# RetNet attention and a gated MLP on one core: the late tokens in blocks of 512, both layers by 26 products, sums of W_out streamed from DRAM

## The chip, the cores and the metric

The kernel runs on one core of a Trainium2 chip. The metric is the device time of one execution, in microseconds. A core has five engines that run their own instruction streams in order and wait for each other by semaphores: TensorE (PE in the profile; PEld are its weight loads), VectorE (DVE), ScalarE (ACT), GpSimd (POOL) and SyncE (SP), which here only issues DMAs. Data lie in SBUF, products land in PSUM, inputs and outputs are in DRAM.

## The reference

```python
# q, k, v: (4, 8, 768, 64) float32; the weights are float64
for t in range(768):
    state = gamma * state + k[:, :, t] (outer) v[:, :, t]     # per head, 64 x 64
    y[:, :, t] = scale * q[:, :, t] @ state
x = y as (3072 tokens, 512)
h = x @ w_in                                   # w_in (512, 2048)
g = h * erf(softplus(h))
out = g @ w_out                                # w_out (2048, 512)
```

All 3072 x 512 outputs are computed in float32. The weights arrive as float64 words and are turned into float32 on the chip.

## The kernel before

Tokens are cut into 24 chunks of 128 (`j`), six to a batch. Attention works by chunks: scores inside a chunk, the state of 64 x 64 per head carried from chunk to chunk. The decays are multiplied into keys and queries beforehand (`prepared`, L575: keys by rows, keys and queries in blocks of 32, then two 32 x 32 block transposes on VectorE).

*The first 512 tokens* (groups g = 0 to 3, G0 = 4) use plain products: `hidden` (L901) makes four feature tiles of 512 columns, `project` (L921) multiplies them by W_out, while VectorE and ScalarE still convert the weights.

*The late 2560 tokens* go in ten pieces of 256 (SCH), each in two halves s of the features: 20 groups g = 4 to 23. In `hidden_steps` (L978) the first layer is a fast product scheme, 26 products in place of 32 (`STEPS`), each as two matmuls of 128 columns; four PSUM banks are read, added into `h` by VectorE (L999) or first written by ScalarE (L1001, L1003), and used again. The sums of x that the products need are made by `x_sums` (L957, 18 a piece), those of W_in once by `sum_in` (L381, 30 a half). The second layer is a seven-product scheme (`PRODUCTS`, `project_part`, L1058): four gated sums a group (`g_sums`, L1040, VectorE), the sums of W_out made once by a ScalarE copy and an accumulating DMA from GpSimd (`sums`, L388), the products gathered in PSUM and combined by `put_part` (L1084). So the order of the late work is written out by hand in the loop at L1266: within a group, 26 steps of the first layer, three output products of the group before among them, then softplus (`gate_softplus`), the visit of one attention chunk (`sub_visit`, L755: its own additions and the scores of the next chunk), erf, four more output products, and gating.

*DMAs.* Everything but the accumulating ones is issued by SP in program order. `load(j)` (L195) brings a late chunk by 34 DMAs: keys and values whole (L208, L218), queries and keys once more as 16 small DMAs of 16 KB each (`load_blocks`, L184, issued at L190), because the block transposes want 32 x 32 blocks in place. `kq` and `v` have three buffers, `kb` two, so the load of chunk j waits until the visit of chunk j - 3 is over. In the loop `load(j + 3)` follows each visit.

```python
for s, d in itertools.product(range(2), range(2)):      # load_blocks, L187 to L193
    part = slice((2 * s + d) * 32, (2 * s + d + 1) * 32)
    for u in range(HP):
        nc.sync.dma_start(to[part, u * C : (u + 1) * C]..., src[2 * u + s, :, d * 32 : (d + 1) * 32]...)
```

Of the kernel before, what the change touches and what calls it, by code (L numbers as in the profile page):

```python
# [22 lines left out]
P = 128  # L23
C = 128
# [9 lines left out]


OUT = {"11": 0, "12": 1, "21": 2, "22": 3, "T3": 1, "T1": 4, "T2": 5, "T4": 6}

PRODUCTS = {
    1: ("11", "11"), 2: ("12", "21"), 3: ("S4", "22"), 4: ("22", "T4"),
    5: ("S1", "T1"), 6: ("S2", "T2"), 7: ("S3", "T3"),  # L40
}

# [60 lines left out]
    (10, 14, 2, True, ((3, True),)),  # L106
    (22, 0, 3, True, ((5, True),)),
    (23, 7, 0, False, ((5, True),)),
    (24, (0, 1), 1, False, ((7, False),)),
    (25, 15, 2, False, ((2, True),)),  # L110
    (14, (2, 1), 3, False, ((7, True),)),
    (9, 8, 0, False, ((7, True),)),
    (12, 6, 1, False, ((6, False),)),
    (2, 11, 2, True, ((2, False), (6, True))),
    (17, 1, 3, True, ((2, False), (4, True))),
    (15, 10, 0, False, ((6, True),)),
    (8, 9, 1, False, ((4, False),)),
    (3, 4, 0, False, ()),
    (19, (1, 0), 0, False, ((0, True),)),
    (7, 13, 1, False, ((2, True),)),  # L120
    (0, 2, 2, False, ((0, True),)),
    (18, 16, 0, False, ((2, False),)),
    (16, 12, 1, False, ((3, True),)),
    (6, (2, 0), 3, False, ((6, True),)),
    (11, (3, 0), 2, True, ((4, True),)),
    (5, 0, 0, False, ()),
    (4, 17, 0, False, ((3, False),)),
    (1, 3, 0, False, ((1, True),)),
    (13, (3, 1), 1, False, ((5, False),)),
)  # L130


# [7 lines left out]
def kernel(  # L140
# [85 lines left out]
    w_out_sb = const.tile([P, 2, 7, FG, DH], F32, name="w_out_sb")  # L226
# [5 lines left out]
    def w_out_of(ft):  # L232
        half, s, i = ft // (2 * FG), ft % (2 * FG) // FG, ft % FG
        return w_out_sb[:, s, 2 * half : 2 * half + 2, i, :]
# [4 lines left out]
    spare = [w_out_sb[:, s, 4:7].rearrange("p a b c -> p (a b c)") for s in range(2)]  # L239
    spare += [w_in_sb[:, s, 16:25].rearrange("p a f -> p (a f)") for s in (1, 0)]  # L240
    later = ret.tile([P, N_X, P], F32, name="xs", bufs=1).rearrange("p a f -> p (a f)")


    LO = slice(2 * CE + 2, 2 * CE + 2 + CE // 2)
    whole_powers = [later[:, i * CE : (i + 1) * CE].bitcast(U32) for i in range(2)]
    powers = [
        [x.bitcast(U16) for x in two] for two in (
            (spare[0][:, LO], spare[1][:, LO]),
            (later[:, : CE // 2], later[:, CE // 2 : CE]),
            (spare[1][:, : CE // 2], spare[1][:, CE // 2 : CE]),  # L250
        )
# [18 lines left out]
    def load_piece(n, *parts):  # L270
# [16 lines left out]
        else:  # L287
            for d in range(2):
                nc.sync.dma_start(
                    w.rearrange("p (d f c) -> p d f c", d=2, f=2)[:, d],  # L290
                    x[i * 2 * P : (i + 1) * 2 * P, d * words * DH : (d + 1) * words * DH].rearrange(
                        "(f p) c -> p f c", p=P
                    ),
                )
# [7 lines left out]
    def whole_conversion(n):  # L302
# [6 lines left out]
        for part, rows in parts:  # L309
            last = n > 0 or rows.start == 1  # L310
            words = spare[place[n]][:, : 2 * CE].bitcast(U32)
            if which == "in":
                f = slice(2 * P) if part is None else slice(part * P, (part + 1) * P)
                fb = 2 * half + at
                to = w_in_sb[:, s, 4 * fb : 4 * fb + 4, f].rearrange("p (h k) f -> p h k f", h=2)
            else:
                to = w_out_sb[:, s, 2 * half : 2 * half + 2, at * 2 : at * 2 + 2, :]
# [31 lines left out]
    def shifted_conversion(n):  # L349
# [7 lines left out]
        if which == "in":  # L357
            fb = 2 * half + at
            to = w_in_sb[:, s, 4 * fb : 4 * fb + 4, :].rearrange("p (h k) f -> p h k f", h=2)
        else:  # L360
            to = w_out_sb[:, s, 2 * half : 2 * half + 2, at * 2 : at * 2 + 2, :]
        up, down = (
            x.rearrange("p (h a b) -> p h a b", h=2, a=2) for x in powers[2 if n == n_p - 1 else n % 2]
# [17 lines left out]
    def sum_in(s, upto):  # L381

        assert all(("hidden", 2 * FG + s * FG + u) in done for u in range(FG))
        for to, a, b, sign in W_SUMS[in_sums[s] : upto]:
            nc.vector.tensor_tensor(w_in_sb[:, s, to], w_in_sb[:, s, a], w_in_sb[:, s, b], op=OP[sign])  # L385
        in_sums[s] = max(in_sums[s], upto)

    def sums(s):  # L388

        assert ("project", s) in done  # L390
        x = {name: w_out_sb[:, s, at] for name, at in OUT.items()}
        for to, a, b in (("T1", "12", "11"), ("T2", "22", "T1"), ("T3", "22", "12"), ("T4", "21", "T2")):
            nc.scalar.activation(x[to], x[b], AF.Copy, scale=-1.0)
            nc.gpsimd.dma_start(x[to], x[a], accum_op=ALU.add)
            done.add((to, s))
            yield
# [15 lines left out]
    def later_sums():  # L412
        for s in range(2):
            yield from sums(s)

    weight_steps = weights()
    last_steps = later_sums()
# [9 lines left out]
    def need(*what):  # L427
        nonlocal room
        while what not in done:
            cost = next(weight_steps, None)  # L430
            if cost is None:
                next(last_steps)
            room -= cost or 0
# [141 lines left out]
    def prepared(j):  # L575

        if j >= NJ:
            return
        nc.vector.tensor_tensor(
            KQ[j][:, 0], KQ[j][:, 0],  # L580
            kq_s[:, j % NC, 0, :, None].to_broadcast([P, H, D]), op=ALU.mult,
        )
        yield
        blocks = (KB[j], KQ[j][:, 1].rearrange("p h d -> p (h d)"))
        for i, x in enumerate(blocks):
            x = x.rearrange("p (u a d) -> p u a d", u=HP, d=32)
            by = kq_b[:, j % NC, i, :, :, None].to_broadcast([P, HP, 4, 32])
            nc.vector.tensor_tensor(x, x, by, op=ALU.mult)
            yield
        for name, store, x in zip("kq", (KT, QT), blocks):  # L590
            store[j] = ret.tile([P, HP, C], F32, name=name + "T")
            nc.vector.transpose(store[j].rearrange("p u t -> p (u t)"), x)
            yield
# [14 lines left out]
    def ret_mask(j):  # L608
        AM[j] = ret.tile([P, 2, HP, C], F32, name="am")
# [64 lines left out]
    def sub_mask(j):  # L674
        AM[j] = ret.tile([P, 2, HP, C], F32, name="am")
        for s in range(2):
            nc.vector.tensor_tensor(  # L677
                AM[j][:, s, :, :D],
# [30 lines left out]
    def sub_results(j):  # L709
# [15 lines left out]
        for crossed in range(2):  # L725
            for u in PAIRS:
                for a in range(2):
# [6 lines left out]
                        AM[j][t, r, u, :D],  # L734
# [20 lines left out]
    def sub_visit(j, g):  # L755

# [13 lines left out]
        def of_state(a):  # L772
            t = slice(a * D, (a + 1) * D)
            for u in PAIRS:
                for r in range(2):
                    col, own = u // 2, slice(r * D, (r + 1) * D)
                    x = state_1 if g == G0 else state
                    nc.tensor.matmul(  # L778
                        pp[r][col * D : (col + 1) * D, u % 2, t], x[own, u, :], QT[j][own, u, t],
# [3 lines left out]


        other = SC[j + 1] = [ret_psum(ps_h) for _ in range(2)]

        def of_values(crossed):
            for u in PAIRS:
                for a in range(2):
# [6 lines left out]
                        AM[j][t, r, u, :D],  # L796
# [5 lines left out]
        last = chunk_of(g - 1)  # L802
        if (g - G0) % 2 == 1:
            clear.update((("o", 0), ("o", 1)))
        new = [
            None if g == G0 else O[last][3][:, 1, :].rearrange("p (u d) -> p u d", d=D),
            pp[1][:, 2:, :].rearrange("p a (b d) -> p (a b) d", d=D),
        ]
        adds = range(int(g == G0), 2 if c < NC - 1 else 1)
        for u in range(HP):  # L810
            for r in range(2):
                for a in adds:
# [3 lines left out]
                        start=first("o" if a == 0 else 1, r), stop=True, skip_group_check=True,  # L816
                    )
        if g > G0 and c:
            nc.vector.tensor_tensor(state, state, new[0], op=ALU.add)
        elif g > G0:  # L820
# [3 lines left out]
        if j + 1 < NJ:  # L824
# [13 lines left out]
        if c < NC - 1:  # L838
            nc.vector.tensor_tensor(state, state_1 if g == G0 else state, new[1], op=ALU.add)
# [16 lines left out]

# [4 lines left out]
    def gate_erf(g):  # L861

        for half in range(2) if g == NG - 1 else (slice(None),):
            if g == NG - 1:
                half = slice(half * N // 2, (half + 1) * N // 2)
            nc.scalar.activation(E[g][:, half], E[g][:, half], AF.Erf)  # L866
# [34 lines left out]
    def hidden(g, u):  # L901
        ft = g * FG + u
        if u == 0:
            HS[g] = act.tile([P, N], F32, name="h")
# [16 lines left out]
    def project(g, tt, part=slice(None)):  # L921
# [8 lines left out]
        for tt, u in of[part]:  # L930
            ft = g * FG + u
            nc.tensor.matmul(  # L932
                O[0][tt].rearrange("p (d c) -> p d c", d=2),
# [454 lines left out]
```

## Time and profile before

| | |
|---|---|
| median of 2 runs | 662.71 us (660.67 and 664.76) |
| span of the profiled execution, first to last instruction | 659.9 us |
| what lies around the span, against the median | 2.8 us |
| TensorE busy | 654.1 us, clock granted 1.00 throughout |
| VectorE, ScalarE, GpSimd busy | 504.4, 289.6, 21.5 us |
| DMA | 51.9 MB, mean 79 GB/s |

The page of the profile has the busy time of each engine, the span in 40 slices, the DMA queues, the chain of work that ended last (followed back from the last instruction to whatever released each step), the costliest groups of instructions and the DMA issues. Further views used here are the chain in order of time, the timeline of one engine or of SP's queue (start, length, line, instruction, how many), and the waits by line. TensorE's instructions overlap, so the time from one start to the next says more than the mean length. DMA issues are not counted as busy, so SP has no line in the table.

### The profile page before, as it was taken

The page shows a single profiled execution, that of the slowest core. Times are in us where ns is not written, and L with a number is a line of the kernel's source. Part 1 is how long each engine was busy: PE and PEld are TensorE (multiplying, and loading weights), DVE is VectorE, ACT ScalarE, POOL GpSimd, SP SyncE. Part 2 cuts the span into 40 slices and gives each one's busy share as a digit, 9 for nine tenths or more (in the row PEclk, how much of TensorE's full clock was granted, in tenths as well). Part 3 has the DMA queues.
Part 4 walks back from the last instruction along what each step waited for, and adds up shares of the span by engine and source line. Part 5 has one row for each costly group of instructions (what it writes and reads, how often), then busy time and mean ns, then how long its engine had stood idle before and what let it go on. Part 6 is the DMA issues. An engine that isn't in the chain of part 4 may idle for free.

```text
span 659.9 us, 15375 instructions
## 1 busy us (share of the span) xinstructions
PE 654.1 (99%) x6240; PEld 556.8 (84%) x6240; DVE 504.4 (76%) x1112; ACT 289.6 (44%) x410; POOL 21.5 (3%) x49
## 2 busy tenths in 40 slices
PE   8999999999999999999999999999999999999998
PEld 7744444487999999999999999999999999999997
DVE  5999879988886886787778678677787788476464
ACT  3468584527625334244254253342432542543440
POOL 1000061101100000000000000000000000000000
PEclk9999999999999999999999999999999999999999
DMA  9999972555843321222222322222231210000000
GB/s 190 222 236 220 211 246 43 107 100 120 165 77 59 79 47 35 68 44 48 68 46 45 73 39 50 60 52 42 38 80 34 45 55 1 1 35 1 1 32 33
DMA packets 157511, 51.90 MB, mean 79 GB/s; under 512 B 141312, under 2 KB 147840, under 8 KB 157440
## 3 DMA queue, kind: packets, MB, share of 16 engines
q1 hardware_dynamic: 155328, 46.71, 33.3%
q0 software_dynamic: 1696, 4.21, 3.4%
q8 instruction: 49, 0.80, 0.5%
q14 instruction: 22, 0.18, 0.1%
q10 hardware_dynamic: 416, 0.01, 0.0%
HBM read 40.39 MB, written 6.29 MB: 71 GB/s over the span
## 4 chain that ended last, share of the span: by engine, by line
PE 95%; DVE 3%; DMA 1%; SPq 0%; issue 0%; ACT 0%
PE o L1070 37%; PE hp L987 23%; PE r L987 12%; PE hp L896 8%; PE o L932 6%; PE r L778 2%; PE hp L670 1%; PE o L814 1%; DMA kq<-in_k_dram 1%; DVE w_in_sb L385 1%; PE r L599 1%; PE o L646 1%; PE r L793 1%; DVE xs L969 1%; PE hp L793 1%; PE r L566 1%
## 5 line engine op out<-in xcount | busy, mean ns | idle before, releaser
L987 PE MATMUL hp<-xs,w_in_sb 128*128 128x128 f32 x1040 | 145.6, 275 | 0.0
L1070 PE MATMUL o<-w_out_sb,h 128*128 128x256 f32 (+1 forms) x640 | 142.7, 380 | 0.0
L987 PEld LDWEIGHTS hp<-xs,w_in_sb 128*128 128x128 f32 x1040 | 135.2, 192 | 4.0 <-issue 0.7
L999 DVE TENSOR_TENSOR h<-h,hp 128x256 f32<-128x256 f32 x200 | 82.1, 419 | 73.6 <-PE hp L987 68.5
L1070 PEld LDWEIGHTS o<-w_out_sb,h 128*128 128x128 f32 x640 | 119.5, 190 | 16.6
L1070 PE MATMUL o<-w_out_sb,e 128*128 128x256 f32 x480 | 113.5, 379 | 0.0
L859 ACT ACTIVATE e<-h 128x2048 f32<-128x2048 f32 x22 | 42.0, 1910 | 120.6 <-DVE h L999 120.6
L1070 PEld LDWEIGHTS o<-w_out_sb,e 128*128 128x128 f32 x480 | 86.8, 190 | 9.4
L999 DVE TENSOR_TENSOR h<-h,r 128x256 f32<-128x256 f32 x160 | 59.9, 416 | 21.7 <-PE r L987 20.6
L1001 ACT COPY h<-hp 128x256 f32<-128x256 f32 x40 | 14.9, 373 | 134.6 <-PE hp L987 106.5
L987 PE MATMUL r<-xs,w_in_sb 128*128 128x128 f32 x480 | 66.7, 275 | 0.4 <-DVE am L677 0.4
L987 PEld LDWEIGHTS r<-xs,w_in_sb 128*128 128x128 f32 x480 | 60.0, 192 | 0.6 <-PE hp L987 0.6
L896 PE MATMUL hp<-xT,w_in_sb 128*128 128x512 f32 (+2 forms) x144 | 56.6, 548 | 0.0
L885 DVE TENSOR_TENSOR e<-h,e 128x1024 f32<-128x1024 f32 x42 | 49.3, 1213 | 8.0 <-ACT e L866 8.0
L987 PE MATMUL hp<-xT,w_in_sb 128*128 128x128 f32 x320 | 48.9, 275 | 0.0
L896 PEld LDWEIGHTS hp<-xT,w_in_sb 128*128 128x128 f32 x144 | 25.7, 190 | 27.2 <-issue 24.6
L987 PEld LDWEIGHTS hp<-xT,w_in_sb 128*128 128x128 f32 x320 | 43.6, 192 | 1.5 <-issue 0.5
L866 ACT ACTIVATE e<-e 128x2048 f32<-128x2048 f32 (+1 forms) x23 | 42.1, 1836 | 0.2
L1003 ACT ACTIVATE h<-hp 128x256 f32<-128x256 f32 x60 | 23.0, 384 | 31.1 <-PE hp L987 29.8
L987 PE MATMUL r<-xT,w_in_sb 128*128 128x128 f32 x240 | 33.3, 275 | 0.0
L866 ACT ACT_TABLE_LOAD x24 | 30.8, 1283 | 0.4
L987 PEld LDWEIGHTS r<-xT,w_in_sb 128*128 128x128 f32 x240 | 30.0, 192 | 0.0
(176 smaller groups left out, 778.6 us busy)
## 6 DMA issues: line engine op xcount, KB each, us to landing
w_out_sb<-in_moe_w_out_dram SPq DMA_DIRECT2D x14, 512.0 KB, 7.8
kq<-in_k_dram SPq DMA_DIRECT2D x23, 256.0 KB, 4.0
v<-in_v_dram SPq DMA_DIRECT2D x23, 256.0 KB, 3.4
out_dram<-r SPq DMA_DIRECT2D x23, 256.0 KB, 2.7
kq<-in_q_dram SPq DMA_DIRECT2D x288, 16.0 KB, 1.8
kb<-in_k_dram SPq DMA_DIRECT2D x288, 16.0 KB, 1.7
w_in_sb<-in_moe_w_in_dram SPq DMA_DIRECT2D x8, 512.0 KB, 13.2
w_out_sb<-w_out_sb POOLq DMA_DIRECT2D x8, 512.0 KB, 5.1
```

The lines of the kernel that those rows point to most:

```text
L778: nc.tensor.matmul(pp[r][col * D : (col + 1) * D, u % 2, t], x[own, u, :], QT[j][own, u, t], start=first(r, col), stop=True, skip_group_ch ...
L793: nc.tensor.matmul(other[a][own, u % 2, D:] if crossed else pp[a][own, u % 2, t], V[j][t, 2 * u + r, :], AM[j][t, r, u, :D], start=crossed ...
L859: nc.scalar.activation(E[g], HS[g], AF.Softplus)
L866: nc.scalar.activation(E[g][:, half], E[g][:, half], AF.Erf)
L885: nc.vector.tensor_tensor(E[g][:, half], HS[g][:, half], E[g][:, half], op=ALU.mult)
L896: nc.tensor.matmul(HP_[ft][:, t], w_in_of(ft, kk), XC[0][:, kk, t], start=(kk == 0), stop=(kk == n_k - 1),)
L932: nc.tensor.matmul(O[0][tt].rearrange("p (d c) -> p d c", d=2), E[g][:, u * TCH + tt * P : u * TCH + (tt + 1) * P], w_out_of(ft), start=(f ...
L987: nc.tensor.matmul(to[:, u, :], w_in_sb[:, s, w, u * P : (u + 1) * P], XS[m](x), start=first and u == 0, stop=True, skip_group_check=True,)
L999: nc.vector.tensor_tensor(h, h, of, op=ALU.add if plus else ALU.subtract)
L1001: nc.scalar.copy(h, of)
L1003: nc.scalar.activation(h, of, AF.Copy, scale=-1.0)
L1070: nc.tensor.matmul(O[m][i][:, half, at], G[g][a][:, u * P : (u + 1) * P], w_out_sb[:, s, OUT[b], u, at], start=i not in started, stop=(s = ...
```

## The change

- The late tokens go in five blocks of 512 (m = 1 to 5), each with two halves s and, in the first layer, two tiles u: four units of 26 products of 256 columns.
- The second layer uses the same scheme of 26 products with the roles exchanged (`project_steps`): the gated values are summed by the 30 sums of `W_SUMS` (`gated_sums`), on GpSimd; W_out is summed by the 18 sums of `X_SUMS` once (`out_sums`, half by accumulating DMAs, the rest on GpSimd), stored to DRAM (24 blocks of 256 KB for each s) and streamed back, 26 blocks for every m and s, through a ring of 11 places in SBUF. Each product's result is added into the output rows `R` by VectorE. Only block 1, s = 0, uses plain products (`project_plain`).
- The decays of the keys go to the values: `prepared` multiplies V by rows (for chunks 6 to 11 on ScalarE, head by head) instead of keys by rows and keys by blocks.
- softplus, erf and gating go in quarters of 512.
- The order of all late instructions is written out as strings of letters (`FIRST`, `STEADY`, `LAST`), one letter for the next step of a stream: h first layer, p second layer, v visits, l one DMA of a chunk's load, r preparing, w gated sums, o W_out sums, x sums of x, s and t sums of W_in, a softplus and erf, g gating, n the first ring loads.
- `w_out_sb` becomes the ring and room for gated sums after block 1; `h` becomes one tile `h_sb` of four units; the converted weights are staged there.

```diff
+CW = 512
+LAST_VECTOR = 12
+BY_ACT = range(6, 12)
+FIRST = (
+    "r l r l r2 l2 r l3 r l o2 l4 o2 l o r l6 o l4 o l5 g l s o s l s l2 s3 l s l p2 g s r s3 p s7 r3 "
+    "p s p2 r p l p l3 p l s p l s p l p f s r s p l2 r l s l p s l s p l p l s p l v l2 p l6 p r2 l2 "
...
+STEADY = (
+    (
+    "w5 h w v h w h w15 h2 w h l w l2 w l w l h l h l h r l h2 l h2 l2 h l r h2 l h2 w l8 r l4 h l3 h3 "
...
-    def sums(s):
...
-            nc.scalar.activation(x[to], x[b], AF.Copy, scale=-1.0)
-            nc.gpsimd.dma_start(x[to], x[a], accum_op=ALU.add)
...
+    def prepared(j, by_act=False):
...
+        if by_act:
+            for h in range(0, H):
+                nc.scalar.activation(V[j][:, h, :], V[j][:, h, :], AF.Copy, scale=kq_s[:, j % NC, 0, h : h + 1])
...
+            nc.vector.tensor_tensor(
+                V[j], V[j], kq_s[:, j % NC, 0, :, None].to_broadcast([P, H, D]), op=ALU.mult,
+            )
...
+    def hidden_steps(m, i):
...
+            to = banks[bank][:, :SCH]
...
+            nc.tensor.matmul(
+                to, w_in_sb[:, s, w, u * P : (u + 1) * P], XS[m](x),
+                start=first, stop=True, skip_group_check=True,
+            )
...
+    def out_sums(s, space, order, transfers=()):
...
+        def put(x):
+            nc.sync.dma_start(w_dram[s, KEYS.index(x)].rearrange("p (v c) -> p v c", v=2), of(x))
...
+            nc.gpsimd.tensor_tensor(of(to), of(a), of(b), op=OP[sign])
...
+    N_RING = 11
...
+    def load_next():
+
+        n = next(loaded)
+        if n < len(stream):
+            s, x = stream[n]
+            nc.sync.dma_start(ring[n % N_RING], w_dram[s, KEYS.index(x)].rearrange("p (v c) -> p v c", v=2))
...
+    def gated_sums(m, s):
+
+        for n, (to, a, b, sign) in enumerate(W_SUMS):
...
+            engine = nc.vector if (m, s) == (NM - 1, 1) and n < LAST_VECTOR else nc.gpsimd
+            engine.tensor_tensor(g_block(s, to, m), g_block(s, a, m), g_block(s, b, m), op=OP[sign])
+            yield
...
+    def project_steps(m, s):
...
+            g, tile_of = g_block(s, w, m), ring[next(used) % N_RING]
+            for v in range(2):
+                nc.tensor.matmul(
+                    of, g[:, v], tile_of[:, v],
+                    start=first and v == 0, stop=v == 1, skip_group_check=True,
+                )
+            load_next()
+            for o, plus in reads:
...
+                if s or o in written:
+                    nc.vector.tensor_tensor(r, r, of, op=ALU.add if plus else ALU.subtract)
...
+    def late_load(j):
...
+        for to, src in ((KQ[j][:, 0], k), (V[j], v)):
+            nc.sync.dma_start(to, src[b, :, now, :].rearrange("h p d -> p h d"))
+            yield
+        for to, src in ((KQ[j][:, 1].rearrange("p h d -> p (h d)"), q), (KB[j], k)):
+            for s, d, u in itertools.product(range(2), range(2), range(HP)):
+                nc.sync.dma_start(
...
-    for g in range(G0 + 1, NG):
...
-            if j + 3 < NJ:
-                load(j + 3)
...
+    def emit(script):
+        for word in script.split():
+            for _ in range(int(word[1:] or 1)):
+                next(streams[word[0]], None)
+
+    emit(FIRST)
+    for m in range(2, NM - 1):
+        for script in STEADY:
+            emit(script)
+    for script in LAST:
+        emit(script)
```

681 lines of the change are left out of this document (357 added, 324 removed), and 22 rows, old and new, of tables (FIRST, LAST, STEADY).

## The prediction

> **What bounds the kernel now.** Read first the page's busy table and its chain of work that ended last, then the chain in order of time, then the load queue (SP) on its own timeline.
>
> ```profile
> PE 654.1 (99%) x6240; PEld 556.8 (84%) x6240; DVE 504.4 (76%) x1112; ACT 289.6 (44%) x410; POOL 21.5 (3%) x49
> ...
> PE 95%; DVE 3%; DMA 1%; SPq 0%; issue 0%; ACT 0%
> ```
>
> TensorE bounds it: 95% of the chain. Its prices come from the chain in order of time (start, length, instruction, count), because the mean of one instruction in the groups (275 ns for 128 columns) overlaps its neighbour's:
>
> ```profile
> 228.07 7.10 PE o L1070 x32
> 235.18 0.89 PE hp L987 x8
> ...
> 241.43 1.73 PE o L1070 x8
> ```
>
> A float32 product is two instructions. Eight of 128 columns take 0.89, so a product is 0.2225 us; the 56 of 256 columns in one group take 7.10 + 3 x 1.73 = 12.29, so a product is 0.439. The load queue has no line in the busy table; its timeline shows what the page hides:
>
> ```profile
> 94.38 0.46 SPq L208 DMA_DIRECT2D kq<-in_k_dram  x1
> ...
> 122.83 9.66 SPq L190 DMA_DIRECT2D kb<-in_k_dram  x16
> 132.53 0.47 SPq L218 DMA_DIRECT2D v<-in_v_dram  x1
> 133.05 0.58 SPq L208 DMA_DIRECT2D kq<-in_k_dram  x1
> ...
> 155.49 11.11 SPq L190 DMA_DIRECT2D kq<-in_q_dram  x16
> 166.70 10.28 SPq L190 DMA_DIRECT2D kb<-in_k_dram  x16
> 177.07 0.38 SPq L218 DMA_DIRECT2D v<-in_v_dram  x1
> ```
> ```profile
> 226.99 0.39 SPq L208 DMA_DIRECT2D kq<-in_k_dram  x1
> 227.44 8.92 SPq L190 DMA_DIRECT2D kq<-in_q_dram  x16
> 236.40 8.32 SPq L190 DMA_DIRECT2D kb<-in_k_dram  x16
> 244.82 0.39 SPq L218 DMA_DIRECT2D v<-in_v_dram  x1
> 252.91 0.38 SPq L208 DMA_DIRECT2D kq<-in_k_dram  x1
> ```
>
> One chunk of 128 tokens is 34 DMAs, and issuing them occupies the queue for 18.2 us (226.99 to 245.2), whatever the DMA engines do; only then does it sit idle, 7.7 us, until a buffer comes free. The wait list says the same (us in total, times, longest):
>
> ```profile
> SPq L208 <- PE r L814: 71.6, 11, 8.8
> ```
>
> From 94 to 219 us the queue is never idle and a chunk takes 17.5 to 22.6 us. So today one chunk per 25.9 us group uses 70% of this queue; it is about as near a bound as VectorE with its 76%.
>
> **The change part by part.** *First layer.* 1040 products of 128 columns (1040 x 0.2225 = 231.4 us) become 520 of 256 (x 0.439 = 228.3): minus 3.1. The arithmetic is the same, 26 products for 32. *Second layer.* 560 products of 256 (7 for 8; 245.8) become 468 of 256 (205.5) and 32 plain ones of 512 columns in the first block (24 instructions of L896 take 10.51, so 0.876 each: 28.0): minus 12.3. The 64-column products of the attention, 2.0 us a chunk, stay. TensorE's own work falls by 15.4 us, all of it on the path.
>
> *VectorE*, per 512 tokens (two of the old chunk pairs, 103.7 us, of which it is 76% busy, 79). Added: 44 additions of products into the output rows, 256 wide; L385 does ten such in 3.93, so 44 x 0.39 = 17.2. Removed: 16 gated sums of 512 (0.61 apart in the chain: 9.8), the four output steps of each half (2.4 x 2 = 4.8), one of five preparing operations a chunk (2.4), and half the x-sum instructions (36 of 128 at 0.27 become 18 of 256 at 0.39: 2.7). Gating in 512s instead of 1024s adds 0.5. Sum minus 2: still about 77 us beside some 99 us of TensorE, hidden; uncovered it would cost nothing new. *ScalarE*: softplus and erf in quarters, 32 x 0.58 = 18.6 for 15.3 a block, plus 3 for first writes and 48 head-wise value scalings (0.2 each by its one-column row, 10 us in all); it stays below half busy. Hidden by TensorE's products.
>
> *GpSimd*: 60 gated sums of 256 columns a block, which no row shows. Its sums of 8 and 32 columns take 285 and 326 ns, 1.7 ns a column, so 0.71 us at 256. Bounds: VectorE's 0.42 for the same shape, and 326 x 8 = 2.6. I take 0.71, the slope of its own rows. 60 x 0.71 = 43 us of 99, and before the first output product of a group needs its 9th to 14th sum TensorE has 26 first-layer products and a visit, 26 x 0.439 + 2.0 = 13.4 us, against 14 x 0.71 = 10. Cost nothing; above 0.96 us a sum TensorE waits.
>
> *Contention.* Nothing in this trace has GpSimd summing beside VectorE. The Trainium skill, SBUF — State Buffer, Who interferes with whom, says that a VectorE instruction with two SBUF inputs and a reading GpSimd instruction exclude each other for a whole instruction. By that rule the some 42 such VectorE instructions of a block would wait up to half a GpSimd sum each, an estimate of 15 us a block, still below TensorE's time.
>
> *The load queue* is where the change lands. It gains 48 stores of W_out sums and 234 loads of 256 KB (52 a block), none of which waits for more than the product 11 before. By the output rows (two in 0.94) each holds the queue 0.47 us. A block of 512 tokens is then 4 x 18.2 + 56 x 0.47 = 99 us of issuing against 208 x 0.439 + 4 x 2.0 = 99 us of products: two queues of one length, and in places each waits for the other. It is hidden no longer.
>
> It is worse at the start. A block now needs four chunks visited before its first product, not two, so the order wants chunks 8 to 13 within 96 us of TensorE work (127.8 to the scores of chunk 13, and the queue is free from 133): 16 us each, where today each has 25.9. The loads cannot move ahead: up to chunk 7 the queue is as today, never idle from 94 us, and ends that chunk with v at 133.0. Then, in the order of the built program:
> - chunk 9: 2 x 18.2 + 8 stores and 2 outputs x 0.47 = 41.1, landed (1.7 more) at 175.8. TensorE, four 512-column products of the first tokens' output further back than today when it begins the scores of chunk 6 (131.3 today, 127.8 then), has 16 such products (14.0), 26 of 256 (11.4) and 160 small ones (64 make a visit's 2.0, so 5.3) up to the scores of chunk 9: 158.5. It waits 17 us there; behind the scores stand the rest of visit 8 and all products after it. VectorE waits too, on the transposes of the keys, with the additions that free the PSUM banks behind them.
> - chunk 14: 7 x 18.2 + 63 x 0.47 = 157.0, landed at 291.7; its scores come 106 products of 256 (46.5), 32 of 512 (28.0) and 304 small ones (10.0) behind those of chunk 9, at 243.0 without any wait. Lag 49 us.
> - chunk 23, the last: 16 x 18.2 + 178 x 0.47 = 374.9, landed at 509.6, transposed at 510.3. TensorE then still has 236 + 166 products of 256 columns and 104 small: 176.5 + 3.4 = 179.9. End 690.2, and 3.0 for the last output as today: span 693.
>
> Two more terms. While stores and accumulations moved data, chunks 8 to 11 took 20.3, 22.6, 21.2 and 17.5 us today, 8.8 above 4 x 18.2; the new stage has the same accumulations' halves and 12.6 MB of stores: plus 8.8. And each ring load waits for the product 11 before, so the queue is held in turn by a TensorE that is 49 us late: by the same sums it reaches the 90th ring load at 449 and TensorE, without lag, the product before it at 406, only 43 apart; plus 6. Span 708; 2.8 lie around it (median 662.7 over span 659.9; the two runs are 660.7 and 664.8): 710.5.
>
> One rule speaks against this sum. The Trainium skill, DMA: Bandwidth & Descriptors, Issuing engines are not separate DMA queues, says that the time to initiate a DMA is usually small relative to the DMA itself. By that rule the queue would not matter and the result would be rival B's. For the 16 KB loads the trace disagrees: 0.47 to 0.6 us of queue against 1.8 us to landing, with several in flight.
>
> **The rivals.**
> A, the forecast: the load queue sets the pace, 710.
> B, the other side: the queue keeps ahead and TensorE's work decides. 659.9 - 15.4 + 2.8 = 647. For it: 95% of the chain is TensorE, and VectorE covers as before. Against it: chunk 9 is in time only if two chunks are issued in 158.5 - 1.7 - 133.0 - 4.7 = 19.1 us, 0.28 us a load where the rows have 0.52 to 0.56. From there on it decides.
> C, the queue at its best: 0.474 us a small load with nothing lost after the big ones and 0.44 for the others. A chunk is 16.0, and chunk 14 lands at 133 + 112 + 28 + 1.7 = 274.7 instead of 291.7, lag 32; afterwards the queue keeps up. At most 647 + 32 = 679; I take 677, since a little of the 5% of the chain that is not TensorE's today would be waited through at the same time. For it: the small loads that start at 229.76, 230.24 and 230.71 do stand 0.475 apart. Against it: behind every 256 KB load the next two take 2.2 us (227.44 to 229.7).
> D: GpSimd's sums are late, at 1.5 us by exclusion or by price. 14 x 1.5 = 21 against 13.4 leaves 7.6 us in each of nine groups: 647 + 68 = 715 without any load lag. For it: sums hang on each other. Against it: 0.71 by its rows, and a late load gives it time.
>
> **How the numbers follow.** A 0.64, B 0.09, C 0.17, D 0.10. Time 710. Range: down to C's side, 666; up to every chunk at today's dearest 22.6 (16 x 4.4 = 70 more in the queue, of which congestion above already has 9): 710 + 61 is the far bound, and since slower blocks also thin the traffic I take two thirds, 752. Below it lies B, 0.09; the rest of 2 in 10 lies beyond both ends. Two per cent, about what a measurement of this kernel can tell from no change, is 649.5 to 676. Faster: most of B, 0.07. Same: the rest of B and, as its time lies on the border, half of C with some of A's low end, 0.13. Slower: 0.80.
>
> **What would show it.** The load queue's timeline without idle time from 94 us to about 510, small loads 0.47 to 0.6 us apart, and in its waits no PE r but its own transfers. TensorE idle 10 to 20 us before the scores of chunk 9, about 50 in all up to chunk 14, then little; VectorE's longest waits on transfers of kq and kb, in the transposes. TensorE's busy time near 640, 256-column products 0.22 us an instruction apart. The last 170 us without such waits. GpSimd's sums near 0.7 us. I am wrong if TensorE's idle time stays below 15 us (B), if it ends before chunk 14 (C), or if the idle time is put down to GpSimd's sums (D).

## The result, and the profile after

The changed kernel takes 738.72 us (two runs, 738.36 and 739.07) against 662.71: ratio 1.116, 95% interval 1.109 to 1.123. Its profiled execution spans 736.7 us, 76.8 more than before's 659.9. The forecast was 710 with a range of 666 to 752.

From the page of the changed kernel: busy times, the granted clock in 40 slices of the span, and the chain that ended last.

```profile
PE 665.8 (90%) x5072; PEld 500.9 (68%) x5072; DVE 508.5 (69%) x1127; ACT 313.0 (42%) x583; POOL 259.4 (35%) x334
...
PEclk9999999889899887799999999999999999999999
...
PE 52%; SPq 15%; DVE 13%; DMA 10%; ACT 5%; issue 4%; POOL 1%; DVEq 0%; ACTq 0%; POOLq 0%
```

TensorE was 95% of the chain and is now 52%; the load queue's own issuing (SPq), which was at 0%, is 15%, VectorE 13% instead of 3, transfers 10% instead of 1. The clock row is new too: it was 9 throughout. The load queue's timeline (start, length, instruction, count) for the tenth chunk (9), and where the loads of chunks 19 to 23 begin and end:

```profile
161.54 0.39 SPq L1241 DMA_DIRECT2D kq<-in_k_dram  x1
162.04 0.52 SPq L1241 DMA_DIRECT2D v<-in_v_dram  x1
162.61 2.85 SPq L1245 DMA_DIRECT2D kq<-in_q_dram  x5
165.57 0.61 SPq L968 DMA_DIRECT2D out_dram<-r  x1
166.23 5.83 SPq L1245 DMA_DIRECT2D kq<-in_q_dram  x11
172.16 4.65 SPq L1245 DMA_DIRECT2D kb<-in_k_dram  x10
176.91 0.56 SPq L968 DMA_DIRECT2D out_dram<-r  x1
177.52 4.16 SPq L1245 DMA_DIRECT2D kb<-in_k_dram  x6
181.78 0.39 SPq L1241 DMA_DIRECT2D kq<-in_k_dram  x1
...
413.92 0.38 SPq L1241 DMA_DIRECT2D kq<-in_k_dram  x1
...
523.70 0.38 SPq L1241 DMA_DIRECT2D kq<-in_k_dram  x1
...
546.40 0.43 SPq L1245 DMA_DIRECT2D kb<-in_k_dram  x1
546.93 19.70 SPq L1111 DMA_DIRECT2D w_out_sb<-w_dram  x19
```

A chunk occupies the queue for 20.2 us. Four chunks with their ring loads and outputs take 109.8 (413.92 to 523.70) where the forecast had 99, and the last chunk is issued at 546.8 instead of 507.9. From 94 us up to there the queue never pauses for more than 1.4 us. In the wait list of the changed kernel (total, times, longest) the queue hardly waits for chunk buffers any more: no wait before a chunk's loads is longer than 1.2 us, where before had 71.6 us in all. Where it waits, it is for the products whose ring slots it refills, and 123.0 of these 131.7 us lie behind 547 us, where TensorE hardly waits:

```profile
SPq L1111 <- PE o L1181: 131.7, 121, 14.4
```

The table of stages of the changed kernel: window, then busy time and instructions of PE, PEld, DVE, ACT, POOL, granted clock, DMA share, GB/s.

```profile
133.00:160.00 27.00, 16.77 (x229) 9.53 (x228) 13.30 (x33) 6.33 (x23) 2.63 (x2) 0.76 0.49 127
160.00:180.00 20.00, 16.75 (x57) 11.37 (x56) 15.79 (x42) 5.52 (x17) 2.49 (x2) 0.90 0.41 84
180.00:220.00 40.00, 31.39 (x369) 21.15 (x367) 26.24 (x62) 13.65 (x31) 13.15 (x10) 0.91 0.58 160
220.00:260.00 40.00, 28.35 (x215) 19.04 (x215) 16.72 (x38) 20.46 (x43) 18.05 (x14) 0.91 0.57 170
260.00:300.00 40.00, 33.22 (x314) 23.24 (x313) 29.89 (x65) 14.31 (x30) 18.36 (x25) 0.83 0.44 100
300.00:340.00 40.00, 34.24 (x267) 29.14 (x266) 25.39 (x61) 12.73 (x25) 4.55 (x6) 0.91 0.59 153
```

In these windows before's TensorE was busy throughout (26.6 of 27.0 us in the first, all of the others) at clock 1.00. A busy share overstates its work here, because instructions at a lower clock last longer. So for all kernels below its work is also counted thus: every matmul instruction with the median step (start to the next start) of its shape in the kernel before, 0.112 us for 128 columns, 0.216 for 256, 0.429 for 512.

```
work in us, by stage            0-94   94-340   340-580   580-end   all
before                          83.1    232.8     228.5      75.3   619.8
changed kernel                  82.2    162.1     205.3     149.4   599.1
```

The work fell by 20.7. From 94 to 340 us TensorE did 70.7 less than before in the same time, from 340 to 580 another 23.2: 93.9 lost, 20.7 saved, 73 of the 76.8. The early stage is three quarters of the loss.

### The profile page after: what moved, and what is told of

Read it like the earlier page. It is cut to its first block, busy times and chain, and to the rows that moved or that the text cites. A ratio compares the mean times of both kernels' runs of the same rounds, so it can differ in the third digit from the quotient of the medians.

```text
span 736.7 us, 14386 instructions
## 1 busy us (share of the span) xinstructions
PE 665.8 (90%) x5072; PEld 500.9 (68%) x5072; DVE 508.5 (69%) x1127; ACT 313.0 (42%) x583; POOL 259.4 (35%) x334
## 4 chain that ended last, share of the span: by engine, by line
PE 52%; SPq 15%; DVE 13%; DMA 10%; ACT 5%; issue 4%; POOL 1%; DVEq 0%; ACTq 0%; POOLq 0%
PE o L1181 22%; PE o L1023 10%; PE hp L1023 9%; SPq L1245 7%; PE r L1023 5%; SPq L226 4%; DMA w_out_sb<-w_dram 4%; DVE h_sb L1031 3%; DMA kb<-in_k_dram 2%; DVE xs L998 2%; PE o L1156 1%; DMA w_in_sb<-in_moe_w_in_dram 1%; DMA kq<-in_q_dram 1%; SPq L248 1%; PE hp L698 1%
## 5 line engine op out<-in xcount | busy, mean ns | idle before, releaser
L1181 PE MATMUL o<-w_out_sb,h_sb 128*128 128x256 f32 x576 | 140.0, 381 | 9.7 <-DMA w_out_sb<-w_dram 7.9
L1181 PEld LDWEIGHTS o<-w_out_sb,h_sb 128*128 128x128 f32 x576 | 107.8, 190 | 30.2 <-DMA w_out_sb<-w_dram 4.2
L1190 DVE TENSOR_TENSOR r<-r,o 128x256 f32<-128x256 f32 x202 | 82.0, 416 | 56.8 <-PE o L1181 53.7
L1023 PE MATMUL hp<-xs,w_in_sb 128*128 128x256 f32 x312 | 90.4, 394 | 13.2 <-ACT h_sb L1033 9.1
L1139 POOL TENSOR_TENSOR h_sb<-h_sb 128x256 f32<-128x256 f32 x116 | 85.3, 748 | 26.9 <-DVE h_sb L1226 22.8
L1181 PE MATMUL o<-w_out_sb 128*128 128x256 f32 x320 | 81.9, 385 | 2.9 <-DMA w_out_sb<-w_dram 2.1
L1031 DVE TENSOR_TENSOR h_sb<-h_sb,hp 128x256 f32<-128x256 f32 x120 | 49.7, 417 | 43.2 <-PE hp L1023 23.0
L1023 PEld LDWEIGHTS hp<-xs,w_in_sb 128*128 128x128 f32 x312 | 59.9, 196 | 28.7 <-ACT h_sb L1033 12.1
L1023 PE MATMUL o<-xs,w_in_sb 128*128 128x256 f32 x304 | 75.5, 393 | 1.7 <-DVE h_sb L1031 1.4
L1226 DVE TENSOR_TENSOR h_sb<-h_sb,e 128x512 f32<-128x512 f32 x80 | 62.6, 793 | 13.4 <-ACT e L1218 13.4
L1031 DVE TENSOR_TENSOR h_sb<-h_sb,o 128x256 f32<-128x256 f32 x144 | 55.5, 415 | 21.2 <-PE o L1023 14.4
L1181 PEld LDWEIGHTS o<-w_out_sb 128*128 128x128 f32 x320 | 60.4, 192 | 13.5 <-DVE r L1190 2.9
L1023 PEld LDWEIGHTS o<-xs,w_in_sb 128*128 128x128 f32 x304 | 56.5, 194 | 14.7 <-DVE h_sb L1031 6.2
L1031 DVE TENSOR_TENSOR h_sb<-h_sb,r 128x256 f32<-128x256 f32 x96 | 37.6, 413 | 11.4 <-PE r L1023 10.0
```

What stands on the lines that cost most here:

```text
L1023: nc.tensor.matmul(to, w_in_sb[:, s, w, u * P : (u + 1) * P], XS[m](x), start=first, stop=True, skip_group_check=True,)
L1031: nc.vector.tensor_tensor(h, h, of, op=ALU.add if plus else ALU.subtract)
L1139: engine.tensor_tensor(g_block(s, to, m), g_block(s, a, m), g_block(s, b, m), op=OP[sign])
L1181: nc.tensor.matmul(of, g[:, v], tile_of[:, v], start=first and v == 0, stop=v == 1, skip_group_check=True,)
L1190: nc.vector.tensor_tensor(r, r, of, op=ALU.add if plus else ALU.subtract)
L1226: nc.vector.tensor_tensor(HS[m, i][:, a], HS[m, i][:, a], E[m, i][:, a], op=ALU.mult)
```

## The experiments

Each kernel is the changed one with the edit shown, timed in three rounds beside the kernel before (661 to 662 us in all of them). Each expectation gives every theory its own range of times, called its range below.

**Queues of single transfers.** Four edits to what SP issues.

```diff
-            nc.sync.dma_start(ring[n % N_RING], w_dram[s, ...
+            nc.scalar.dma_start(ring[n % N_RING], w_dram[s, ...
```


> Only the 234 loads of W_out sums into the ring are issued by ScalarE's queue instead of SP's. If SP's issue time sets the pace (the forecast), SP's block of four chunks falls from 108 us (chunk 15 begun at 306.3, chunk 19 at 413.9) by 52 x 0.42 = 22 us to 86, below TensorE's 99: the lag no longer grows after chunk 14, and before it 11 loads (5 us) go; 690 to 710 us. If the ring loads themselves are what is late (each waits for the product 11 before, then lands 2 to 4 us later), they come no earlier behind ScalarE's activations: 730 us or more. If only TensorE's lowered clock or GpSimd decides, no change, 733 to 745.

Measured 768.74, 30 us slower than the changed kernel. Only the open range "730 us or more" takes it in, and that stood for loads that come no earlier, not for a loss. Each ring load waits for a product, and on ScalarE's queue everything behind it waits too. ScalarE's timeline in that kernel, with its idle time before and what ended it in square brackets:

```profile
339.94 4.67 ACTq L1111 DMA_DIRECT2D w_out_sb<-w_dram  x3
344.69 1.28 ACT L1218 ACT_TABLE_LOAD   x1 [7.70 <-DVE r L1190]
...
352.03 3.50 ACTq L1111 DMA_DIRECT2D w_out_sb<-w_dram  x3
355.95 0.37 ACT L1033 COPY h_sb<-o 128x256 f32<-128x256 f32 x1 [4.04 <-DMA w_out_sb<-w_dram]
```

The activation stood behind 4.7 us of ring loads and the first layer's copies behind 3.5. This run tells what the move costs, not what SP's time is worth.

```diff
-                nc.sync.dma_start(
+                (nc.scalar if src is k else nc.sync).dma_start(
                     to[(2 * s + d) * 32 : (2 * s + d + 1) * 32, u * C : (u + 1) * C]...
```


> Of the 32 small loads of each chunk from the ninth on, the 16 of kb are issued by ScalarE's queue instead of SP's. If SP's issue time sets the pace, SP has 18 DMAs a chunk, seven chunks (8 to 14) lose about 7 x 8 = 56 us of queue, the lag of 63 us at chunk 14 shrinks to under 15, and a block is 4 x 10 + 56 x 0.45 = 65 us: 655 to 685 us, unless ScalarE is delayed by its 256 issues of 0.43. If the ring loads' lateness decides, they stay on SP in the same order: above 715. If the lowered clock is a cause of its own and no consequence of the waits, at most 10 us are won.

721.00: 17.7 won, at most a third of what the issue-time theory said. The number lies in the range for late ring loads (above 715), and more was won than the 10 us of the theory on the clock. SP ran ahead (chunk 14's share issued at 287 instead of 306), but the other share was issued by ScalarE only at 288, and these issues stood in ScalarE's own way, as in the run before (a copy of the first layer at 161.85 us behind 4.2 us of three issues). So the run does not settle what the issue time of these loads is worth.

```diff
-            nc.sync.dma_start(w_dram[s, KEYS.index(x)]..., of(x))
+            nc.gpsimd.dma_start(w_dram[s, KEYS.index(x)]..., of(x))
```


> The 48 stores of W_out sums are issued by GpSimd's own queue, behind the sum that they store, instead of SP's. The issue-time theory: 48 x 0.45 = 22 us leave SP before chunk 14, and with them SP's waits for GpSimd's sums (9 us together with those for ScalarE): chunk 14 lands 25 to 30 us earlier, 705 to 715 us. A rival: SP, the stores and GpSimd's sums wait for one another in a ring (a sum waits for the store that frees its space, the store for its place in SP, SP for the sum), and TensorE waits behind them because the first layer's fourth block is written over that space (9.1 us before 256.9): then more is won than SP's issue time, below 700. If stores are hidden: 733 or more.

725.91: 12.8 won, 11 short of the nearest range. The groups of VectorE from 127 to 180 us show one place where the rest can have gone. Columns: line, engine, operation, shapes, count, then busy us and mean ns:

```profile
L423 DVE TENSOR_TENSOR w_in_sb<-w_in_sb 128x256 f32<-128x256 f32 x31 | 23.2, 781 | 0.2
```

GpSimd's additions, no longer held up by SP, now ran beside VectorE's W_in sums, and these took 781 ns instead of the 422 of before, 11 us for the 31 of them. Beside that, copies of the first layer waited 19.3 us for GpSimd's sums, 14.7 in the changed kernel; no run separates the two.

```diff
-        if n < len(stream):
+        if n < N_RING:
```


> Ring loads are left out after the first 11, so later products of the second layer read old W_out sums (57 MB less traffic, and no product waits for a load). Issue-time theory: the same as with the ring loads on another queue, 690 to 710. If the transfers or their latency cost by themselves (chunk loads on a busier set of DMA engines, products waiting 2 to 4 us for a load), it is clearly faster than that kernel, by 15 us or more. If neither matters: 733 or more.

722.39: 16.3 won, between the ranges (690 to 710, 733 or more). It is 46 us faster than the run with the ring loads on ScalarE, but that one lost by what stood behind them. In the count of work 161.0 from 94 to 340, about as before this edit, but 220.7 from 340 to 580 instead of 205.3: in the later stage the ring loads cost something, by their issue or by coming late, and the early loss, most of it before the first of the loads left out, has another reason.

**Leaving out what fills the queue.**

```diff
-        KB[j] = loads.tile([P, HP * C], F32, name="kb", bufs=2)
+        KB[j] = KB[6 + j % 2]
...
-            for s, d, u in itertools.product(range(2), range(2), range(HP)):
-                nc.sync.dma_start(
...
+            if src is q:
+                nc.sync.dma_start(KQ[j][:, 1], q[b, :, now, :].rearrange("h p d -> p h d"))
```


> From the ninth chunk on a chunk is 3 loads of 256 KB instead of 34: q in one piece in the wrong layout, and the keys' blocks of chunks 6 and 7 are used again. Stores and ring loads stay. If the number of chunk loads in SP's queue is what delays the early stage, the 71 us that TensorE loses there between 94 and 340 us shrink to under 25 and the 24 us lost from 340 to 580 go too: 650 to 675 us. If the ring of stores, GpSimd's sums and SP is the cause, it stays: 710 to 728. If it is the order itself (VectorE's W_in sums, x sums and transposes in one queue), above 700 as well, and the two are told apart by the next two kernels.

702.54: 36.2 won, and no more, in the range for the order of the work (above 700). 31 of 34 loads a chunk are gone, and VectorE's wait for kb in the early stage falls from 17.8 to 4.2 us, which are left for chunks 6 and 7, whose loads stay. The later stage is nearly whole (work of 223.7 for 228.5) with all ring loads in place, so there they were late because of the chunk loads ahead of them. But from 94 to 340 us TensorE did 178.7 of 232.8.

```diff
-            nc.sync.dma_start(w_dram[s, KEYS.index(x)]..., of(x))
+            pass
...
-        if n < len(stream):
+        if n < 0:
```


> All 48 stores and all 234 ring loads are left out (GpSimd's sums of W_out stay, the products read old weights); the chunk loads stay as they are. The queue then holds 34 loads a chunk and the outputs: by 18.2 us a chunk the one after the fourteenth is landed at 133 + 7 x 18.2 + 2 = 262 instead of 309, 19 us behind TensorE's own 243: 665 to 690 us. If the chunk loads alone are enough to hold everything up: 705 to 722, no better than without ring loads. If the ring of stores and sums is the whole cause: below 660.

707.74: 31.0 won, in the range for "the chunk loads alone are enough to hold everything up". The next run takes that reading away. Both edits together:

> Both: three loads a chunk, no stores, no ring loads. What is left of the loss is neither chunk loads nor stores. If the load queue is the cause, TensorE's own work decides: 636 to 652 us, and the granted clock stays at 1.00. If the order of the work on VectorE, ScalarE and GpSimd is the cause, or the clock falls by itself: 690 or more.

706.97. With three loads a chunk, no stores and no ring loads it is no faster than with the better of the two edits alone, and 45 us slower than before. This is the run against the forecast: the queue is nearly empty and TensorE still waits. The groups of this kernel from 133 to 165 us, VectorE's first, then GpSimd's:

```profile
L423 DVE TENSOR_TENSOR w_in_sb<-w_in_sb 128x256 f32<-128x256 f32 x21 | 27.8, 1363 | 0.2
```
```profile
L1093 POOL TENSOR_TENSOR h_sb<-w_out_sb,h_sb 128x512 f32<-128x512 f32 x8 | 11.7, 1468 | 0.4
L1093 POOL TENSOR_TENSOR h_sb<-w_out_sb 128x512 f32<-128x512 f32 x8 | 11.5, 1462 | 0.1
L1093 POOL TENSOR_TENSOR h_sb<-h_sb 128x512 f32<-128x512 f32 x7 | 9.5, 1360 | 0.4
```

Without stores to wait for, GpSimd adds without a pause, and nearly every W_in sum of VectorE takes as long as one GpSimd addition: 1.36 us in the mean, alone 0.42.

> GpSimd's 148 gated sums are left out (the second layer's products read unsummed blocks). If they come late or slow VectorE enough to be felt, at least 15 us are won: below 724. If they are hidden, as forecast: 731 to 743.

```diff
-            engine.tensor_tensor(g_block(s, to, m), g_block(s, a, m), g_block(s, b, m), op=OP[sign])
+            if engine is nc.vector:
+                engine.tensor_tensor(g_block(s, to, m), g_block(s, a, m), g_block(s, b, m), op=OP[sign])
```

738.82: nothing won. The 258 gated sums on GpSimd (the trace counts these, the expectation had 148) are hidden, and so is the contention that they bring.

**Leaving out GpSimd's additions for the W_out sums.** The changed kernel has 28 of them (the expectations say 26); the other 8 of the 36 sums, and not half, are accumulating DMAs. The edit stands in all three runs: first with the edits of the 706.97 kernel, then alone, then with the three loads a chunk.

```diff
-            nc.gpsimd.tensor_tensor(of(to), of(a), of(b), op=OP[sign])
+            pass
```


> As the kernel with three loads a chunk and neither stores nor ring loads (707 us), and GpSimd's 26 additions for the W_out sums are left out too. There, VectorE's additions of two SBUF inputs took 1.48 us beside a GpSimd sum and 0.42 alone, 27 of 60 W_in sums, 25 us in all, on the chain from 127 to 165 us. If the queue and this contention together are the loss: 645 to 660 us. If contention is only its 25 us and the rest is the order of the dependent work on VectorE and ScalarE (at 271 to 286 us activation, gating, x sums and transposes follow one another while TensorE waits): 675 to 690. If contention is beside the point: 700 to 710.

685.30, 21.7 less than with these additions, in the range for contention as one part and the order of the work as the rest: in the same place the W_in sums take their 0.42 again.

```profile
L423 DVE TENSOR_TENSOR w_in_sb<-w_in_sb 128x256 f32<-128x256 f32 x22 | 8.7, 416 | 0.1
```


> Only GpSimd's 26 additions for the W_out sums are left out; chunk loads, stores (of whatever stands there) and ring loads stay. Contention cost the changed kernel only some 16 us in all VectorE instructions, most of it hidden. If the queue alone sets its pace: 728 to 742 us, unchanged. If the ring of sums and stores and SP is a loss of its own (a sum waits for the store that frees its space, 95 us in all, the first layer waits behind it 9.1 us): 705 to 725.

734.85: 3.9 won, hardly clear of the scatter (733.4 to 739.3). Alone the additions cost almost nothing: in the changed kernel they wait 95.2 us for their stores in the slow queue, and only 3 of VectorE's 60 W_in sums overlap one. The rival that sums, stores and SP waiting for one another are a loss of their own (705 to 725) is out.

> Three loads a chunk and no GpSimd additions for the W_out sums; stores and ring loads stay. With both causes of the early stage gone and the steady stage relieved: 650 to 670 us if queue and contention or the ring of stores are all there is; 680 to 700 if the order of the dependent work is the rest. It must then stand within 10 us of the kernel with nothing in the queue and no such additions.

686.98, with all stores and ring loads in place: within 2 us of the 685 us kernel, which has neither, as expected if the order of the work is the rest (680 to 700). So stores and ring loads do little harm once the chunk loads are few and these additions gone.

**What is left.** The chain of the 685 us kernel in order of time, at a block's boundary, and then the line of TensorE's timeline that ends it:

```profile
246.84 1.07 PE o L1156 x2
...
248.53 1.28 ACT L1218
249.83 2.19 ACT e L1218 x4
...
254.46 0.69 DVE h_sb L1226
255.15 1.20 DVE xs L998 x2
256.35 2.27 DVE h_sb L1226 x2
258.62 1.73 DVE xs L998 x2
...
260.95 0.62 DVE kT L618
261.57 0.60 DVE qT L618
262.22 1.13 PE hp L698 x32
```
```profile
262.22 1.13 PE L698 MATMUL hp<-qT,kT 64*64 64x64 f32 x32 [5.07 <-DVE qT L618]
```

Activation, gating, x sums and the transposes of the next chunk follow one another on two in-order engines for 14 us; TensorE has products up to 257.15 and then stands 5.07 us before the scores. The changed kernel has the same stretch from 276.5 to 290.8, with the same 5.07. And its ScalarE, which now scales the values of chunks 6 to 11, stands before those of chunk 7:

```profile
124.62 2.01 ACT L603 ACTIVATE v<-v,kq_s 128x64 f32<-128x64 f32 x8
140.69 2.02 ACT L603 ACTIVATE v<-v,kq_s 128x64 f32<-128x64 f32 x8 [14.05 <-DMA v<-in_v_dram]
142.61 0.56 ACT L967 COPY r<-o 128x512 f32<-128x512 f32 x1
```

Behind it is queued the copy that frees the accumulators; TensorE's next product waits 6.2 us for that copy. The last kernel takes this wait and part of VectorE's W_in sums from the 685 us kernel:

```diff
+            load_values(j)
             load_blocks(KQ[j][:, 1].rearrange("p h d -> p (h d)"), q[b, :, now, :])
             load_blocks(KB[j], k[b, :, now, :])
...
-            (engine or nc.vector).tensor_tensor(
+            if to >= 16:
+                nc.vector.tensor_tensor(
```


> As the kernel with nothing in the queue and no additions for the W_out sums (685 us), with two more things: v of chunks 6 and 7 is loaded before their small loads, and 34 of VectorE's 60 W_in sums are left out. There ScalarE stood 13.3 us before the scaled values of chunk 7, for v, with the copies that free the accumulators queued behind it, and TensorE had 8 us of gaps between 123 and 143 us: with v early these go, 677. The W_in sums stood for 5 to 6 us on the chain between 150 and 192 us and 14 us of VectorE's time in all. If what is left is the order, single waits one after another: both together 668 to 674. If VectorE is simply full in this stage: 14 more, below 662. If the value load is hidden anyway and only the granted clock (0.91 to 0.93 there) is left: above 680.

681.82: 3.5 won, 8 to 14 less than expected of single waits. The number lies in the range for a value load that is hidden and a clock that alone is left (above 680), but that reading does not hold either: the wait for v is gone, and by the trace's clock records TensorE was busy at half clock for only 10.5 us from 94 to 340, an estimate of 5 us. The next wait shows in place of the one for v, first on ScalarE, then on TensorE:

```profile
130.53 0.59 ACT L969 COPY r<-o 128x512 f32<-128x512 f32 x1 [2.60 <-PE o L956]
140.99 1.13 PE L700 MATMUL hp<-qT,kT 64*64 64x64 f32 x32 [4.34 <-DVE qT L620]
```

The copy that stood behind the values at 142.61 now runs at 130.53, but TensorE stands before the scores for the transposes of chunk 7, whose small loads are issued by 138 us here and by 137 in the changed kernel. VectorE with 34 sums fewer (range: below 662 if it is full) changes little either: it is not full, it is late.

## Why the prediction was right and where it was wrong

*Right: the direction, and the queue as a cause.* The queue is issuing from 94 to 547 us. Of the 576 small loads 512 hold it for less than 0.5 us, and from start to start those of q take 0.60 us on average, those of kb 0.53. Leaving out most of them is worth 36 us. How much of that is their issue and how much their transfers, no run separates. TensorE's own work fell, by 20.7 against a forecast of 15.4, and it did not decide. The way of the loss is the forecast's too: VectorE stands before the transposes of a late chunk, and TensorE behind the additions that VectorE then has to do. For chunk 14, VectorE's timeline and then TensorE's:

```profile
308.78 0.71 DVE L618 STREAM_TRANSPOSE kT<-kb 128x512 f32<-128x512 f32 x1 [5.85 <-DMA kb<-in_k_dram]
310.19 2.08 PE L1023 MATMUL o<-xT,w_in_sb 128*128 128x256 f32 x4 [5.76 <-DVE h_sb L1031]
```

*The idle time: the amount right, partly by luck.* By the table of stages TensorE is idle for 46.3 us from 133 to 340 us, 48.8 from 94 on; the forecast had about 50 up to chunk 14. But the wait of 10 to 20 us before the scores of chunk 9 is not there, the nearest is 3.1 us at 185.7. Of the six waits over 3 us, those of 3.7, 3.1 and 5.8 stand behind late chunk loads; 6.2 goes back to a value load, 9.1 to a store's turn in the queue, and 5.1 to the order on ScalarE and VectorE. And the work lost in this stage, 70.7, is 22 more than the idle time: TensorE was also slow while it was busy (see the clock below), for which the forecast had no term.

*The size of the queue's terms was off.* Chunk 9 was issued by 181.7 and not by 174.1, chunk 23 by 546.8 and not 507.9; the scores of chunk 14 began at 315.7, not at 291.7. A block takes 108 to 110 us of queue, not 99. In the block from 413.92 on, the chunk loads hold it 79.6 us instead of 72.8, the ring loads and outputs 30.1 instead of 26.3; the 16 loads of q, now right behind two 256 KB loads, take up to 12.2 us (524.76 to 536.95), where the forecast's row had 8.9. By the last chunk that makes 38.9 us, of which the forecast's 8.8 for congestion and 6 for the ring cover 14.8. The last stretch, from the last chunk's issue to the end, took 189.9 us (forecast 185.3), which with the other 24.1 gives the 28.7 between span 708 and 736.7. That sum is arithmetic and no cause, and the near agreement of the last stretch is in part luck: the forecast starts it with the scores of chunk 23 right behind their load, and they began at 571.3, with TensorE busy in between. From 340 to 580 us the first entry of TensorE's wait list is the ring loads, 9.9 us in 15 waits.

*Wrong: "the queue keeps ahead and TensorE's work decides", 647.* The step under it failed: that the work of ScalarE and VectorE is hidden by TensorE's products. It was an average over a block, and it nearly holds from 340 us on (in the 685 us kernel 225.2 us of work up to 580, before 228.5). In the early stage it doesn't: with next to nothing in the queue 707, with GpSimd's additions out as well 685, 38 above that floor. Of the 91.7 us between 647 and 738.7, in this order of leaving out, 36.2 went with 31 of 34 loads a chunk; another 15.6 with the W_out additions (702.54 to 686.98), 1.7 with stores and ring loads, 3.5 with the values and the W_in sums. Left are 35 us, among them the waits for chunk 7's keys and at the block's boundary, which no run took away one by one; how they divide stays open. So the number 710 was near for partly the wrong reason: the forecast put the whole early loss down to a queue that shares it with contention, the order of the work and a slower clock.

*A step that was not asked.* The 48 scalings of values on ScalarE were costed by their length (0.2 each; 8 took 2.0, so 0.25) and as hidden. What stood before them, a load that ended at 140, and behind them, the copy that frees the accumulators, was not looked at. The wait is 14.05 us on ScalarE and 6.2 on TensorE.

*Contention, hidden as forecast, but a bound in waiting.* The estimate was 15 us a block. In the changed kernel VectorE's instructions that overlap a GpSimd sum are longer than their like alone by 14 to 19 us in the whole execution, by how an overlap is counted, a fifth to a quarter of the estimate. Gating has 8.6 of it: 33 instructions of 0.946 us against 0.685. Leaving the gated sums out gave nothing. But the early W_out additions against W_in sums were second behind the queue and became first as soon as the stores left SP. By the Trainium skill, SBUF — State Buffer, Who interferes with whom, a VectorE instruction with at most one input in SBUF, outside the two-port modes, does not contend with GpSimd: the runs agree, since VectorE's additions with one input in PSUM (L1031, L1190) took 0.41 to 0.42 beside GpSimd and alone.

*A rule weighed and a rival closed.* The forecast set aside the Trainium skill's sentence that the time to initiate a DMA is usually small relative to the DMA itself (DMA: Bandwidth & Descriptors, Issuing engines are not separate DMA queues). For one load it is so here too, 0.43 us of queue against a median of 2.0 to 2.4 to landing; but 34 loads a chunk follow one another, and leaving out 31 won 36.2 us. GpSimd's gated sums take 0.73 us in the median, in groups up to 0.96 in the mean (forecast 0.71, limit 0.96), and without them the time is 738.8: that rival is out. The queue at its best (677) is out by the block's 108 us.

*What would show it.* "In its waits no PE r" held nearly (3.6 us in 9 waits, before had 71.6), "but its own transfers" did not: it waits for products, stores for GpSimd (4.7 us) and outputs for VectorE (9.3). VectorE's waits in the transposes came up to 340 us to 17.8 us for kb, beside 18.2 for first-layer products; TensorE's busy time is 665.8 and not near 640.

## What to carry to other kernels

When several in-order streams are well filled (here VectorE at 69% and a load queue that hardly pauses), leaving out one cause shows only its lead over the next: here 31.7 us for the whole queue, 21.7 more for additions that alone were worth 3.9. Leave suspects out singly and together before giving a floor. And an engine that is "hidden" on average must be followed through the stage where the order is rebuilt: for each instruction moved onto an in-order engine, ask what it waits for and what stands behind it.

## What was not expected of the hardware

The granted clock fell in the stage where TensorE waited, to 0.76 in 133 to 160 us and 0.83 in 260 to 300, while it is 1.00 in the same windows before. After a wait of 9.1 us its timeline in the changed kernel reads:

```profile
246.37 0.59 PE L1023 MATMUL r<-xs,w_in_sb 128*128 128x256 f32 x2
246.80 1.02 PE L1156 MATMUL o<-w_out_sb,h_sb 128*128 128x512 f32 x2
256.92 1.22 PE L1023 MATMUL hp<-xs,w_in_sb 128*128 128x256 f32 x2 [9.10 <-ACT h_sb L1033]
257.94 1.06 PE L1023 MATMUL hp<-xT,w_in_sb 128*128 128x256 f32 x2
258.79 1.91 PE L1156 MATMUL o<-w_out_sb,h_sb 128*128 128x512 f32 x2
```

Pairs of the same shapes are 1.06 and 1.91 long that were 0.59 and 1.02. Worked out from the table of stages, busy time times what is missing of the clock (16.77 x 0.24 + 16.75 x 0.10 + 31.39 x 0.09 + 28.35 x 0.09 + 33.22 x 0.17 + 34.24 x 0.09), an estimate of 20 us of the early loss is this slower clock. The trace's own clock records give 17: TensorE was busy at half clock for 34.7 us between 94 and 340. The Trainium skill, TensorE: Matmul & The Clock Gate, What's actually happening, says that an idle window of about 3.4 us halves the clock; the doubling after a 9.1 us wait agrees. The forecast had no such term. It seems to follow the waits (over the whole span the clock is 0.965 in the changed kernel, 0.98 in the three-load kernel and 0.99 in the 685 us kernel, where TensorE waits less), but no run changed the clock by itself.

The wait of 9.1 us in these lines is another of the queue's by-ways: the copy into the hidden block waited for a GpSimd addition on the same space, that one for the store which frees its place, and the store for its turn in SP. Leaving the additions out alone took it away and won 3.9 us at most, because other waits took its place.
